# A limit on loads under way, block-key scores in one matmul per head, and one-matmul fillers in an attention and MLP kernel

## The chip, the cores and the metric

The kernel runs on one core of a Trainium2 chip. The metric is device time in microseconds, the median of several executions. One more execution is recorded by the hardware profiler; all views below are of that one.

## The reference

Local attention is followed by a gated MLP and a second MLP, all in float32, with 2 batches, 8 heads, 768 positions and a head size of 64. Each query sees the keys nearer than 16 positions and, beside them, 24 block keys (the maximum over each block of 32 keys) with block means of the values:

```
k_sum = k.reshape(B, H, nb, block, D).max(axis=3)
v_sum = v.reshape(B, H, nb, block, D).mean(axis=3)
scores_l = where(|i - j| < window, scale * q @ k.T, -1e9)
scores_s = scale * q @ k_sum.T + log(block)
a = softmax(concat([scores_l, scores_s]))
x = a @ concat([v, v_sum])                    # to 1536 tokens of 512
xn = x / sqrt(mean(x * x) + 1e-6) * rms_g
x = (silu(xn @ w_gate) * (xn @ w_val)) @ w_out          # 512 -> 1536 -> 512
out = (s * relu(x @ w_in) ** 2 + b) @ w_out2            # 512 -> 2048 -> 512
```

## The kernel before

**Attention.** The 2 x 768 queries are 12 tiles of 128 queries, and a tile is two halves of 64 queries (index c), so that each half needs one window of 96 keys. For a tile `do_qk` (L513) computes all scores: 8 heads are 4 pairs (index j) on the two halves of the partitions (index g), and a head's row holds 96 key columns and 24 block-key columns. Per pair it issues four 64x64 matmuls over the key columns (two g by two c) and then four 64x64 ones over the block-key columns (`km`), which all go to the two PSUM banks of g (L522). Then, for each g, DVE adds the mask and takes the maximum (`do_top`, L541), ACT takes the exponential (L548), PE transposes the result (L559), ACT copies it out of PSUM (L569), PE multiplies with the values (L578), and ACT, GpSimd and DVE divide by the sum (L587 to L596). Each tile ends with its RMS norm (L611 to L619), transposes (L627) and a split into a high and a low F32R part (L638, L640).

**Loads.** All loads are issued by SP on one queue, in order: `load_k` (L273, four strips of keys a batch), `load_q` (L440, one a tile, three buffers), `load_v` (L277, the value windows), `load_vt` (L290, values for the block means), `spread_v` (L312, copies of the block means within SBUF), `load_small` (L157) and `w_load` (L199, raw weights as 64-bit words into three buffers). DVE reduces K strips to `km` (L284) and the value strips to block sums (L294). Output stores are at L860.

**Weights.** Each unit of weights is rebuilt from its 64-bit words by ACT and DVE (L205, L214 to L216) and split into high and low F32R parts (L227, L231). The matmuls of the MLPs take three products of these (L726, L727, L730, and L849 to L852).

**Order.** `plan` (L429) lists the attention work, the first nine weight units and the first matmuls of the gated MLP as tasks with a cost, dependencies and a rank; `give_out` (L328) walks a modelled clock and issues on each engine, as it comes free, the ready task of the lowest rank. That fixes each engine's order when the program is built; on the chip each engine runs its order as semaphores allow. Where the modelled PE would idle for more than `IDLE`, four transposes of the identity into a free bank are issued as a filler (L413 and L414). After the plan the rest of the MLPs follows in a fixed loop order (`moe`, L762). In the model SP runs ahead of the loads by at most `AHEAD` (L380), which sets the place of loads in the order, and no wait.

Of the kernel before, what the change touches and what calls it, by code (L numbers as in the profile page):

```python
# [11 lines left out]
I32 = mybir.dt.int32  # L12
# [6 lines left out]
NB, NH, SEQ, HD = 2, 8, 768, 64  # L19
# [5 lines left out]
NS = SEQ // BLK  # L25
HQ = 64
VH = 66
KW = HQ + 2 * WIN
KC = KW + NS
# [6 lines left out]
NSUB = NB * SEQ // SUB  # L36
TPS = SUB // 128
HEAD = 3
LAT = 0.09
AHEAD = 4.0  # L40
IDLE = 0.6
PTENG = ("ACT",)
QB = 3
# [11 lines left out]
def kernel(ctx: ExitStack, tc: tile.TileContext, q_t, k_t, v_w, v_t, w_gate, w_val, w_out, w_in2, w_out2, vecs, out):  # L55
    nc = tc.nc
# [44 lines left out]
    ident = const.tile([128, 128], F32, name="ident")  # L101
# [4 lines left out]
    vec = const.tile([128, DM + 2], F32, name="vec")  # L106
    gbc, sbc, bbc = vec[:, 0:DM], vec[:, DM:DM + 1], vec[:, DM + 1:DM + 2]
    junk = const.tile([128, DM], mybir.dt.bfloat16, name="junk")
    qc = [const.tile([128, NPAIR, 2, HQ], F32, name=f"q{i}") for i in range(QB)]
# [8 lines left out]
    vt0 = xyp.tile([128, 2 * KD * SUB], F32, tag="xy", name="vt")  # L118
# [4 lines left out]
    kst = [t[:, 0:NPAIR * KL].rearrange("p (j s) -> p j s", j=NPAIR) for t in kb]  # L123
    vst = [[t.rearrange("p (s h d) -> p s h d", s=NTL, h=NH) for t in ts]
           for ts in ([t[:, 0:VT] for t in vb], [part[:, i * VT:(i + 1) * VT] for i in range(2)])]
    km = [const.tile([128, NPAIR, NS], F32, name=f"km{b}") for b in range(NB)]
# [21 lines left out]
    def consts_mask2():  # L148
# [3 lines left out]
        for i, p0, o in ((0, 0, 0), (2, 64, HQ + WIN)):  # L152
            nc.gpsimd.tensor_copy(masks[i], m)
            nc.gpsimd.memset(masks[i][p0:p0 + 64, o:o + WIN], NEG / scale)

    def load_small():
        nc.sync.dma_start(out=vec, in_=vecs)  # L157


    later = [[] for _ in range(8)]  # L160
# [22 lines left out]
    units = []  # L183
# [12 lines left out]

    def w_load(i):
        t = rawp.tile([128, 512, 2], I32, tag="raw", name="raw")
        nc.sync.dma_start(out=t.rearrange("p f c -> p (f c)"), in_=units[i].bitcast(I32))  # L199
        raw_t[i] = t  # L200

    def w_scale(i):
# [67 lines left out]


    def load_k(b, j):
        nc.sync.dma_start(out=kst[b][:, j], in_=k_t[b, j])  # L273

    def load_v(b, s0, n):
        t = vst[b][s0 // NTL][0:KW, s0 % NTL:s0 % NTL + n]
        nc.sync.dma_start(out=t.rearrange("p s h d -> p (s h d)"), in_=v_w[b, s0 // n])  # L277

    def ones_v(b, s0, n):
        rows = KC if s0 < (4 if b == 0 else 2) else KW  # L280
# [6 lines left out]
    vs = vt0[:, NPAIR * SEQ:NPAIR * SEQ + 512]  # L287

    def load_vt(b, j):
        nc.sync.dma_start(out=vt0[:, j * SEQ:(j + 1) * SEQ], in_=v_t[b, j])  # L290

    def sum_vt(b, j):
        c0 = j * 128 + KW
# [15 lines left out]
    def spread_v(b, s0, n):  # L309
        a = vst[b][0][KW:KC, 0:2].rearrange("p (o e) h d -> p o (e h d)", o=1).broadcast_to([NS, n // 2, 2 * NH * VH])  # L310
        o = vst[b][s0 // NTL][KW:KC, s0 % NTL:s0 % NTL + n]
        nc.sync.dma_start(out=o.rearrange("p (o e) h d -> p o (e h d)", e=2), in_=a)  # L312


    tasks = []
# [12 lines left out]
    def give_out():  # L328
        count = {k: 0 for k in rings}
        freed = {k: 0 for k in rings}  # L330
        done_at = {k: [] for k in rings}
        bank_free = [(0.0, i) for i in range(8)]
        used_caps = {k: [] for k in caps}
        pending = {e: [] for e in ("PE", "DVE", "ACT", "POOL", "SP")}
        for i, t in enumerate(tasks):
            pending[t["eng"]].append((t["rank"], i, t))
        for p in pending.values():
            p.sort(key=lambda z: z[:2])
        clock = dict.fromkeys(pending, 0.0)
        dma = 0.0  # L340
        now = 0.0
        left = len(tasks)

        ends = {k: {} for k in rings}

        def ring_ok(k):
            n = rings[k]
            c = count[k]
            return c < n or (c - n in ends[k] and ends[k][c - n] <= now)

        while left:
            moved = False
            for e in ("SP", "PE", "ACT", "DVE", "POOL"):
                if clock[e] > now + 1e-9:
                    continue
                for z in pending[e]:
                    t = z[2]
                    if any(d["end"] is None or d["end"] + LAT > now + 1e-9 for d in t["deps"]):
                        continue
                    if not all(ring_ok(k) for k in t["take"]):  # L360
                        continue
                    b = None
                    if t["bank"]:
                        if sum(1 for x in used_caps[t["bank"]] if x["freed"] is None or x["freed"] > now) >= caps[t["bank"]]:
                            continue
                        ok = [x for x in bank_free if x[0] <= now]
                        if not ok:
                            continue
                        b = min(ok)
                        bank_free.remove(b)  # L370
                        t["b"] = b[1]
                        t["freed"] = None
                        used_caps[t["bank"]].append(t)
                    t["slot"] = {}
                    for k in t["take"]:
                        t["slot"][k] = count[k]
                        count[k] += 1
                    if e == "SP":
                        dma = max(dma, now + 0.5) + t["us"]
                        clock[e] = max(now + 0.06, dma - AHEAD)  # L380
                        t["end"] = dma + 1.3
                    else:
                        clock[e] = now + t["us"]
                        t["end"] = clock[e] + (0.06 if e == "PE" else t["more"])
                    for k, o in t["give"]:
                        ends[k][o["slot"][k]] = t["end"] + LAT
                    for o in t["free"]:
                        o["freed"] = t["end"] + LAT
                        bank_free.append((o["freed"], o["b"]))
                    t["at"] = now  # L390
                    if b is not None:
                        t["fn"](b[1])
                    else:
                        t["fn"]()
                    pending[e].remove(z)
                    left -= 1
                    moved = True
                    break
            if moved:
                continue  # L400
            nxt = [c for c in clock.values() if c > now + 1e-9]
            nxt += [x[0] for x in bank_free if x[0] > now]
            nxt += [v for k in rings for v in ends[k].values() if v > now]
            nxt += [t["end"] + LAT for t in tasks if t["end"] is not None and t["end"] + LAT > now + 1e-9]
            assert nxt, [z[2]["why"] if "why" in z[2] else (e, z[0]) for e in pending for z in pending[e][:3]]
            now = min(nxt) + 1e-6
            at = clock["PE"] + IDLE
            if now > at and any(x[0] <= at for x in bank_free) and ident_at[0]["end"] is not None and ident_at[0]["end"] + LAT < at and pending["PE"]:

                now = at  # L410
                i = min(bank_free)[1]
                ps = bank(i)
                for k in range(4):  # L413
                    nc.tensor.transpose(ps[:, k * 128:(k + 1) * 128], ident, ident)  # L414
                clock["PE"] = now + 0.44

    def dve(n):
# [11 lines left out]
    def plan(x):  # L429
# [7 lines left out]
            K[b, j] = task("SP", mb(128 * KL * 4), lambda: load_k(b, j), rank=rank)  # L437

        def load_q(i):
            nc.sync.dma_start(out=qc[i % QB].rearrange("p j c q -> p (j c q)"), in_=q_t[i])  # L440

        def lq(i, rank, deps=()):
            Q[i] = task("SP", mb(128 * 512 * 4), lambda: load_q(i), deps, rank=rank)
# [60 lines left out]
        box = {}  # L504
        def tile_of(n, i):
            b, t = divmod(i, NTL)
            if i >= 2:
                lq(i, n - 5, [qk[i - QB]] if i >= QB else ())

            def hold(bk):  # L510
                box["S", i, 0] = bank(bk)

            def do_qk(bk):  # L513
                box["S", i, 1] = bank(bk)
                sm_of[i] = smallp.tile([128, 2, NH], F32, tag="sm", name="sm")
                four = [(g, c) for g in range(2) for c in range(2)]
                for j in range(NPAIR):
                    for o, n in ((0, KW), (KW, NS)):
                        for g, c in four:
                            p = slice(64 * g, 64 * g + 64)  # L520
                            k0 = 64 * (2 * t + c)
                            nc.tensor.matmul(box["S", i, g][64 * c:64 * c + 64, j * KC + o:j * KC + o + n], qc[i % QB][p, j, c],  # L522
                                             km[b][p, j] if o else kst[b][p, j, k0:k0 + KW], start=True, stop=True)
            deps = [Q[i], *[KM[b, j] for j in range(NPAIR)], *([qk[i - 1]] if i else ())]
            A0 = task("PE", 0.0, hold, deps, n + 1.2, bank="S")
            A1 = qk[i] = task("PE", 1.25, do_qk, [*deps, A0], n + 1.2, bank="S", take=("sm",))
            box["A0", i] = A1
            return A0, A1

        for n, (i, g) in enumerate(us):  # L530
            b, t = divmod(i, NTL)
# [30 lines left out]
            e = PTENG[n % len(PTENG)]  # L562
# [55 lines left out]
            S = task("POOL", 0.75, do_ss, [R], n - 2)  # L618
# [22 lines left out]
            h = task("ACT", act(512), lambda f=two_x: f(0), [ET], n - 1.2)  # L641
# [27 lines left out]
        for s in range(NSUB):  # L669
            for j in range(HEAD):  # L670
                rk = FR[s] + j * FS
                got = {}
                for k in range(2):
                    ps = []
# [268 lines left out]
```

## Time and profile before

| | us |
|---|---|
| median of 3 runs | 648.09 |
| lowest and highest of them | 647.77, 649.55 |
| the profiled execution, its own time | 647.01 |
| its span between first and last instruction | 645.20 |
| PE busy | 622.8 |
| DVE busy | 378.1 |
| ACT busy | 259.8 |

Attention takes the first 110 us, the first three column blocks of the gated MLP beside it; the MLPs alone take the rest. Engines are PE (matmuls), PEld (weight loads of PE), DVE, ACT, POOL (GpSimd) and SP, whose queue issues the DMAs. "Idle" of an engine is put down to the one that ended it. A view by stretches gives each engine's busy time with the number of its instructions in parentheses, the granted clock of PE (1.00 is 2.4 GHz, 0.50 is 1.2 GHz), the mean busy share of the DMA engines and GB/s.

### The profile page before, as it was taken

The page shows a single profiled execution, that of the slowest core. Times are in us where ns is not written, and L with a number is a line of the kernel's source. Part 1 is how long each engine was busy: PE and PEld are TensorE (multiplying, and loading weights), DVE is VectorE, ACT ScalarE, POOL GpSimd, SP SyncE. Part 2 cuts the span into 40 slices and gives each one's busy share as a digit, 9 for nine tenths or more (in the row PEclk, how much of TensorE's full clock was granted, in tenths as well). Part 3 has the DMA queues.
Part 4 walks back from the last instruction along what each step waited for, and adds up shares of the span by engine and source line. Part 5 has one row for each costly group of instructions (what it writes and reads, how often), then busy time and mean ns, then how long its engine had stood idle before and what let it go on. Part 6 is the DMA issues. An engine that isn't in the chain of part 4 may idle for free.

```text
span 645.2 us, 9632 instructions
## 1 busy us (share of the span) xinstructions
PE 622.8 (97%) x3816; PEld 514.3 (80%) x3816; DVE 378.1 (59%) x731; ACT 259.8 (40%) x524; POOL 141.7 (22%) x159
## 2 busy tenths in 40 slices
PE   5588999999999999999999999999999999999998
PEld 3576788888888888888888888888888888888886
DVE  5469886325851555544556767870388457845532
ACT  2576986334433333212333345542554045404400
POOL 2253856322311111111111111100221022103100
PEclk9889999999999999999999999999999999999999
DMA  9979622003440112221122212230212321210022
GB/s 294 230 264 257 193 60 74 1 1 98 131 130 28 42 63 66 86 61 53 62 65 69 64 65 67 65 100 31 56 46 67 94 62 42 66 61 0 2 98 99
DMA packets 17494, 55.04 MB, mean 85 GB/s; under 512 B 2000, under 2 KB 2256, under 8 KB 17448
## 3 DMA queue, kind: packets, MB, share of 16 engines
q1 hardware_dynamic: 17448, 54.42, 27.7%
q8 instruction: 30, 0.49, 0.3%
q14 instruction: 16, 0.13, 0.1%
HBM read 50.35 MB, written 3.15 MB: 83 GB/s over the span
## 4 chain that ended last, share of the span: by engine, by line
PE 91%; DVE 3%; issue 2%; DMA 1%; ACT 1%; SPq 0%; POOL 0%; POOLq 0%
PE b L726 22%; PE b L730 22%; PE b L727 22%; PE b L852 7%; PE b L850 7%; PE b L849 7%; PE b L559 2%; PE b L522 2%; PE b L578 2%; DMA vt<-in_v_t_dram 1%; PE b L627 1%; DVE vt L294 1%; DVE P L541 0%; DVE km L284 0%; ACT P L548 0%
## 5 line engine op out<-in xcount | busy, mean ns | idle before, releaser
L231 POOL TENSOR_TENSOR wl<-wa,wh 128x512 fp32r<-128x512 f32 x68 | 89.1, 1318 | 389.3 <-ACT wh L227 316.0
L726 PE MATMUL b<-x,wh 128*128 128x512 f32 x288 | 113.7, 395 | 0.1
L727 PE MATMUL b<-x,wl 128*128 128x512 f32 x288 | 112.2, 390 | 0.0
L227 ACT ACTIVATE wh<-wa 128x512 fp32r<-128x512 f32 x68 | 41.5, 627 | 97.2 <-PE b L852 45.5
L730 PE MATMUL b<-x,wh 128*128 128x512 f32 x288 | 77.8, 392 | 0.0
L850 PE MATMUL b<-wl,hg 128*128 128x512 f32 (+1 forms) x196 | 75.1, 385 | 0.0
L849 PE MATMUL b<-wh,hg 128*128 128x512 f32 (+1 forms) x196 | 75.1, 385 | 0.0
L726 PE MATMUL b<-y,wh 128*128 128x512 f32 x192 | 74.7, 389 | 0.0
L727 PE MATMUL b<-y,wl 128*128 128x512 f32 x192 | 74.7, 389 | 0.0
L831 DVE SCALAR_TENSOR_TENSOR b<-u,vec 128x512 f32<-128x512 f32 x48 | 50.7, 1057 | 35.6 <-ACT u L830 35.6
L726 PEld LDWEIGHTS b<-x,wh 128*128 128x128 f32 x288 | 54.1, 188 | 11.3 <-ACT x L638 0.4
L727 PEld LDWEIGHTS b<-x,wl 128*128 128x128 f32 x288 | 54.1, 188 | 10.7
L730 PEld LDWEIGHTS b<-x,wh 128*128 128x128 f32 x288 | 53.5, 188 | 11.0
L726 PE MATMUL b<-hg,wh 128*128 128x512 f32 x144 | 56.0, 389 | 0.0
L727 PE MATMUL b<-hg,wl 128*128 128x512 f32 x144 | 56.0, 389 | 0.0
L751 DVE SCALAR_TENSOR_TENSOR hg<-b,vec,hg 128x512 fp32r<-128x512 f32 x48 | 36.0, 749 | 28.1 <-ACT hg L750 28.1
L852 PE MATMUL b<-wh,hg 128*128 128x512 f32 (+1 forms) x196 | 51.5, 385 | 0.0
L730 PE MATMUL b<-y,wh 128*128 128x512 f32 x192 | 51.3, 389 | 0.0
L216 DVE SCALAR_TENSOR_TENSOR wa<-raw,wa 128x512 int32<-128x512 int32 x68 | 50.0, 735 | 2.0
L750 ACT ACTIVATE hg<-b,vec 128x512 fp32r<-128x512 f32 x48 | 33.0, 687 | 43.0 <-DVE b L831 43.0
L858 DVE TENSOR_TENSOR part<-b,part 128x512 f32<-128x512 f32 (+1 forms) x37 | 24.4, 673 | 43.5 <-PE b L852 43.5
L215 DVE SCALAR_TENSOR_TENSOR wa<-raw,wa 128x512 int32<-128x512 int32 x68 | 47.0, 691 | 2.0
(85 smaller groups left out, 947.2 us busy)
## 6 DMA issues: line engine op xcount, KB each, us to landing
raw<-in_w_out_dram SPq DMA_DIRECT2D x28, 512.0 KB, 3.5
raw<-in_w_in_dram SPq DMA_DIRECT2D x16, 512.0 KB, 4.1
raw<-in_w_gate_dram SPq DMA_DIRECT2D x12, 512.0 KB, 3.6
raw<-in_w_val_dram SPq DMA_DIRECT2D x12, 512.0 KB, 3.6
hg<-in_k_t_dram SPq DMA_DIRECT2D x8, 400.0 KB, 10.0
q<-in_q_t_dram SPq DMA_DIRECT2D x12, 256.0 KB, 7.1
vt<-in_v_t_dram SPq DMA_DIRECT2D x8, 384.0 KB, 8.3
out_dram<-part SPq DMA_DIRECT2D x11, 256.0 KB, 2.0
```

The lines of the kernel that those rows point to most:

```text
L215: lambda: nc.vector.scalar_tensor_tensor(out=ai, in0=hi, scalar=-0x80000000, in1=ai, op0=ALU.bitwise_and, op1=ALU.bitwise_or),
L216: lambda: nc.vector.scalar_tensor_tensor(out=ai, in0=lo, scalar=29, in1=ai, op0=ALU.logical_shift_right, op1=ALU.bitwise_or),
L227: nc.scalar.activation(out=r(h), in_=a_t[i], func=AF.Copy)
L231: nc.gpsimd.tensor_tensor(out=r(lo), in0=a_t.pop(i), in1=high[i], op=ALU.subtract)
L726: nc.tensor.matmul(ps, r(hi[:, kk * 128:(kk + 1) * 128]), xh, start=kk == 0, stop=False)
L727: nc.tensor.matmul(ps, r(lo[:, kk * 128:(kk + 1) * 128]), xh, start=False, stop=False)
L730: nc.tensor.matmul(ps, r(hi[:, kk * 128:(kk + 1) * 128]), r(act(kk, 1)), start=False, stop=kk == 3)
L751: nc.vector.scalar_tensor_tensor(out=r(dst[1]), in0=ps, scalar=bias, in1=dst[0], op0=ALU.add, op1=ALU.subtract)
L831: after(0, lambda u=u, ps=ps: nc.vector.scalar_tensor_tensor(out=ps, in0=u, scalar=sbc[:, 0:1], in1=u, op0=ALU.mult, op1=ALU.mult))
L849: nc.tensor.matmul(acc, gh, r(ws[e][0][:, cs]), start=e == 0, stop=False)
L850: nc.tensor.matmul(acc, gh, r(ws[e][1][:, cs]), start=False, stop=False)
L852: nc.tensor.matmul(acc, r(ge[e][:, 1]), r(ws[e][0][:, cs]), start=False, stop=e == 3)
```

## The change

The three edits are these. Every load that SP issues, and the copies of the block means, go through a new `fetch`, which makes each wait until the fourth one before it has landed (`OUT = 4`); the output stores do not. In `do_qk` the four 64x64 matmuls over the block-key columns of a pair become two, one for each g, with both query halves as 128 weight columns; the key columns stay as they are. A filler becomes one F32 matmul of the identity with itself, repeated to 256 columns, in place of four transposes. Costs and ranks of the planner's tasks are unchanged.

```diff
+OUT = 4
@@
+    sent = []
+
+    def fetch(out, in_):
+
+        d = nc.sync.dma_start(out=out, in_=in_).ins
+        if len(sent) >= OUT:
+            tc.add_manual_dep(d, sent[-OUT].name, mybir.DependencyInfo(mybir.DependencyClass.Sync, mybir.DependencyReason.DATA),
+                              reason="transfers under way")
+        sent.append(d)
+
     def load_small():
-        nc.sync.dma_start(out=vec, in_=vecs)
+        fetch(out=vec, in_=vecs)
...
-        nc.sync.dma_start(out=t.rearrange("p f c -> p (f c)"), in_=units[i].bitcast(I32))
+        fetch(out=t.rearrange("p f c -> p (f c)"), in_=units[i].bitcast(I32))
...
-        nc.sync.dma_start(out=kst[b][:, j], in_=k_t[b, j])
+        fetch(out=kst[b][:, j], in_=k_t[b, j])
...
-                for k in range(4):
-                    nc.tensor.transpose(ps[:, k * 128:(k + 1) * 128], ident, ident)
+                nc.tensor.matmul(ps[:, 0:256].rearrange("p (o c) -> p o c", o=2), ident, ident.rearrange("p (o c) -> p o c", o=1).broadcast_to([128, 2, 128]), start=True, stop=True)
...
-                four = [(g, c) for g in range(2) for c in range(2)]
                 for j in range(NPAIR):
-                    for o, n in ((0, KW), (KW, NS)):
-                        for g, c in four:
-                            p = slice(64 * g, 64 * g + 64)
+                    for g in range(2):
+                        p = slice(64 * g, 64 * g + 64)
+                        S = box["S", i, g]
+                        for c in range(2):
                             k0 = 64 * (2 * t + c)
-                            nc.tensor.matmul(box["S", i, g][64 * c:64 * c + 64, j * KC + o:j * KC + o + n], qc[i % QB][p, j, c],
-                                             km[b][p, j] if o else kst[b][p, j, k0:k0 + KW], start=True, stop=True)
+                            nc.tensor.matmul(S[64 * c:64 * c + 64, j * KC:j * KC + KW], qc[i % QB][p, j, c], kst[b][p, j, k0:k0 + KW], start=True, stop=True)
+                    for g in range(2):
+                        p = slice(64 * g, 64 * g + 64)
+                        nc.tensor.matmul(box["S", i, g][:, j * KC + KW:(j + 1) * KC], qc[i % QB][p, j].rearrange("p c q -> p (c q)"), km[b][p, j], start=True, stop=True)
```

## Rows read from the trace of the kernel before

**Rows 1.** The page: busy time, share and instructions of PE; instruction queue, packets, MB.

```profile
PE 622.8 (97%) x3816; PEld 514.3 (80%) x3816; DVE 378.1 (59%) x731; ACT 259.8 (40%) x524; POOL 141.7 (22%) x159
...
q8 instruction: 30, 0.49, 0.3%
```

**Rows 2.** Stretches: PE, PEld, DVE, ACT, POOL busy, clock, DMA share, GB/s.

```profile
15.00:45.00 30.00, 21.61 (x439) 18.75 (x440) 15.61 (x77) 18.84 (x55) 9.90 (x18) 0.83 0.98 274
45.00:70.00 25.00, 21.19 (x358) 17.12 (x357) 24.62 (x70) 18.26 (x49) 13.20 (x18) 1.00 0.84 227
70.00:110.00 40.00, 40.00 (x584) 32.27 (x583) 32.39 (x124) 33.60 (x95) 24.84 (x32) 1.00 0.32 96
110.00:640.00 530.00, 530.00 (x2346) 439.00 (x2345) 296.20 (x438) 185.74 (x321) 89.89 (x70) 1.00 0.19 61
```

**Rows 3.** The chain that ended last, in order of time: start, us, what.

```profile
20.60 2.25 issue
...
28.26 4.58 issue
...
40.70 0.84 issue
```

**Rows 4.** Stretches that end in the second and third of these waits.

```profile
20.70:28.50 7.80, 5.41 (x125) 4.86 (x126) 4.15 (x31) 5.13 (x18) 2.15 (x8) 0.78 1.04 192
28.50:41.20 12.70, 7.65 (x126) 6.40 (x125) 5.38 (x31) 6.99 (x22) 5.14 (x7) 0.73 1.03 346
```

**Rows 5.** DMA view, instruction packets of 20.1 to 21.7, 30.0 to 31.6, 38.9 to 40.3.

```profile
q8 instruction: 1, 0.02, 4.9%
...
q8 instruction: 1, 0.02, 5.2%
...
q8 instruction: 1, 0.02, 4.6%
```

**Rows 6.** DMA view of 4.9 to 37.6 us: count, KB each, median us to landing.

```profile
hg<-in_k_t_dram SPq DMA_DIRECT2D x4, 400.0 KB, 11.2
q<-in_q_t_dram SPq DMA_DIRECT2D x6, 256.0 KB, 9.2
```

**Rows 7.** Line L273, the K strips issued at 0.73 and at 23.62 us.

```profile
DMA to landing us min/median/max: 3.0/3.0/3.0
...
DMA to landing us min/median/max: 12.5/12.5/12.5
```

**Rows 8.** Timeline of SP's queue: start, us, line, out<-in, count.

```profile
23.62 0.33 SPq L273 DMA_DIRECT2D hg<-in_k_t_dram  x1
```

**Rows 9.** Stretches of low granted clock; columns as in the stages.

```profile
23.30:26.60 3.30, 3.30 (x54) 2.91 (x50) 2.13 (x17) 1.72 (x5) 0.27 (x2) 0.50 1.07 169
...
30.10:36.90 6.80, 4.05 (x35) 3.47 (x35) 2.01 (x11) 2.27 (x7) 1.01 (x1) 0.50 1.03 326
```

**Rows 10.** Timeline of DVE, first block maxima of the second batch.

```profile
43.36 0.94 DVE L284 TENSOR_REDUCE km<-hg 128x24 f32<-128x768 f32 x1
```

**Rows 11.** DMA view of 61 to 72 us, the data queue: packets, MB, share.

```profile
q1 hardware_dynamic: 856, 2.57, 87.2%
```

**Rows 12.** Line L522 in a stretch, scores of one tile: PE, PEld, clock, DMA.

```profile
82.76:84.02 1.26, 1.25 (x64) 1.22 (x64) 1.00 0.00 0
```

**Rows 13.** Timeline of PE, 83.3 to 85.6 us: start, us, line, tile, shapes, count.

```profile
83.63 0.38 PE L522 MATMUL b<-hg,q 64*64 64x96 f32 x8
83.83 0.26 PE L522 MATMUL b<-km,q 64*64 64x24 f32 x8
84.02 0.66 PE L627 MATMUL b<-ident,xn 128*128 128x128 f32 x4
84.61 0.69 PE L578 MATMUL b<-part,PT 120*64 120x66 f32 x16
85.22 0.50 PE L726 MATMUL b<-x,wh 128*128 128x512 f32 x1
```

**Rows 14.** Timeline of PE, two fillers.

```profile
51.86 1.04 PE L414 MATMUL b<-ident 128*128 128x128 f32 x8
```

More of the change, by code (lines that the diff above doesn't have):

```diff
@@ L272, in load_k @@
     def load_k(b, j):
-        nc.sync.dma_start(out=kst[b][:, j], in_=k_t[b, j])
+        fetch(out=kst[b][:, j], in_=k_t[b, j])
     def load_v(b, s0, n):
         t = vst[b][s0 // NTL][0:KW, s0 % NTL:s0 % NTL + n]
-        nc.sync.dma_start(out=t.rearrange("p s h d -> p (s h d)"), in_=v_w[b, s0 // n])
+        fetch(out=t.rearrange("p s h d -> p (s h d)"), in_=v_w[b, s0 // n])
     def ones_v(b, s0, n):
@@ L289, in load_vt @@
     def load_vt(b, j):
-        nc.sync.dma_start(out=vt0[:, j * SEQ:(j + 1) * SEQ], in_=v_t[b, j])
+        fetch(out=vt0[:, j * SEQ:(j + 1) * SEQ], in_=v_t[b, j])
     def sum_vt(b, j):
@@ L311, in spread_v @@
         o = vst[b][s0 // NTL][KW:KC, s0 % NTL:s0 % NTL + n]
-        nc.sync.dma_start(out=o.rearrange("p (o e) h d -> p o (e h d)", e=2), in_=a)
+        fetch(out=o.rearrange("p (o e) h d -> p o (e h d)", e=2), in_=a)
     tasks = []
@@ L439, in load_q @@
         def load_q(i):
-            nc.sync.dma_start(out=qc[i % QB].rearrange("p j c q -> p (j c q)"), in_=q_t[i])
+            fetch(out=qc[i % QB].rearrange("p j c q -> p (j c q)"), in_=q_t[i])
         def lq(i, rank, deps=()):
```

## The prediction

> **What bounds the kernel now.** I read the page first, then the stages, then the chain of waits. PE is busy 97% of the span [rows 1], and the stages show where it is not [rows 2]: from 70 to 640 us it is busy without a gap, so there the end moves only with PE's own work. What PE loses before its tail lies ahead of 70, and behind the first loads it is 8.4 us of the 30 from 15 to 45 and 3.8 of the 25 from 45 to 70, where DVE is busy 24.6 of 25 and sets the pace. So I ask what holds the stretch 15 to 45. In the chain it is mostly "issue", time in which the engine waits for nothing that the profile names: 2.25 us at 20.60, 4.58 at 28.26 and 0.84 at 40.70, 7.67 us together [rows 3].
>
> What is "issue"? Between the first and the second of these waits PE and PEld start 125 + 126 = 251 instructions, between the second and the third 251 again [rows 4]. A pause after a fixed number of instructions looks like a block of program that has not come. Queue 8 moves instructions, 30 packets of 0.49 MB, 16 KB each; with 3816 matmuls and as many weight loads that is one packet for some 255 [rows 1]. One such packet lies at 20.1 to 21.7 us, one at 30.0 to 31.6, one at 38.9 to 40.3 [rows 5]; PE goes on at 22.85, 32.84 and 41.54, each time just over a microsecond behind its packet. The trace does not show when a packet was asked for. If it is when the block before it begins, at 22.85 and 32.84, the next ones stood 7.2 and 6.1 us in line.
>
> In line behind what? From 4.9 to 37.6 us 27 loads and copies are issued (the counts of the view added; two of its rows stand), one per 1.2 us, and q and K take 9.2 and 11.2 us to land [rows 6]: 10 / 1.2, about eight under way. A lone K strip lands in 3.0 us [rows 7]. DMA is busy 0.98 of the time [rows 2], so the loads queue, and I read the instruction packets as queueing with them. The rule in the Trainium skill, "Runtime: NRT & Kernel Launch", section "Instruction fetch mechanics", is that crossing the boundary of a block of 256 instructions is "mostly hidden". The trace agrees on the block's size and differs on the cost, 7.67 us; by the page the limit would bring nothing.
>
> **The change, part by part.**
>
> *Four transfers under way.* A load now waits on SP until the fourth before it has landed. All that is behind it on SP's queue waits too: the loads of q, K, v, v_t and the weights' raw tiles, and the SBUF copies of the block means; for these wait, in turn, PE's scores, DVE's block maxima and sums, and ACT's scaling. Data are not moved later by that as long as the DMA engines have work: they are the bound there. Four are enough if moving four takes longer than one alone takes from issue to landing: 4 x 1.2 = 4.8 us against 3.0 plus one issue of 0.33 [rows 6 to 8]. An instruction packet should meet half the line: 7.2 and 6.1 become some 3.3 us, and with 1.4 for the packet and 1.3 until PE moves, 6.0 us. The second block ran 5.4 us (22.85 to 28.26), but will hold more work, since the scores need a quarter fewer instructions and, below, more time. So I take the three waits to go whole: 7.67 us.
>
> With them goes the slow clock. PE's granted clock is 0.50 (1.2 GHz) from 23.3 to 26.6 and from 30.1 to 36.9, each just behind or within a wait, and PE is busy 3.30 + 4.05 = 7.35 us in these [rows 9]. At 2.4 GHz that would be half: 3.7 us. Together 11.3 us are on offer.
>
> They can't all be had, since next come the loads, which go no faster. The second batch's K strip issued at 23.62 lands 12.5 us later, at 36.1, and DVE reads it at 43.36 [rows 7, 8, 10]: 7.2 us of slack. So the cap is 7.2 us, less what the limit costs in DMA pace. That cost no row shows. From below it is 0 (by the 4.8 above; a gain is excluded, since the engines are full). From above, take 61 to 72 us, where fewer loads are queued and the queue's share is 87% [rows 11] instead of 98% [rows 2], partly since SP had nothing to send: 11 points, or 3.4 of the 31 us from 5 to 36. I take 1.0, nearer the lower end, since SP's own waits explain part of that stretch. Gain: 6.2 us, range 3.8 to 7.2.
>
> The MoE stage loses nothing: it has three raw tiles, so no more than three loads can be under way there. The output stores are not limited.
>
> *Block columns in one matmul.* Per head pair, four 64*64 matmuls over 24 columns become two 64*128 ones; each F32 matmul is two PE instructions and two weight loads, so a tile's scores go from 64 + 64 instructions to 48 + 48. They take 1.25 us a tile now [rows 12]. While the shape stays, PE starts the next group 0.18 us before the last one ends: the key columns end at 83.63 + 0.38 = 84.01, the block columns begin at 83.83. Where the shape changes it is 0.07: the block columns end at 84.09, the 128*128 transposes begin at 84.02; these end at 84.68, the 120*64 matmuls begin at 84.61; these end at 85.30, the 128*128 ones begin at 85.22 [rows 13]. The last pair differs in columns alone and pays as well. So a change of shape costs 0.11 us, and the new code has seven more of them a tile (four into 64*128, three back): 0.77 us. No row shows 64*64 against 64*128. From below: no such cost, and fewer instructions, near 0. From above: each pass over 24 columns with the wide weights takes as long as one of the wide transposes, 0.66 / 4 = 0.165 [rows 13]: two per pair are 0.33 where the narrow group takes 0.19 (83.83 to 84.02), 4 x 0.14 = 0.56 more, 1.3. I take 0.77, since every change of shape in the rows pays its 0.11, and 24 columns are far from 128. The Trainium skill says the same in "TensorEngine Tiling (Array Packing)", section "Key Properties": changing the tiling mode drains the engine; its "Available Configurations" list 64*64 and 64*128 as two modes. The trace agrees where it has a change (0.07 against 0.18), and the rule speaks against this edit.
>
> Where does it count? The scores of tiles 8 to 11, at 70.2, 82.8, 86.3 and 91.5 us (one of four rows alike stands), lie in PE's full stretch [rows 2, 12]: 4 x 0.77 = +3.1 us. Those of tiles 6 and 7 lie where PE idles 3.8 us beside DVE: 0. Those of tiles 1 to 5 (3.9 us) eat of the surplus in the first part, 11.3 - 3.9 = 7.4, still above the cap of 7.2; without that surplus they would cost up to 3.9. Tile 0 waits for its loads anyway.
>
> *Fillers.* 13 fillers of four transposes become one F32 matmul of 256 columns, two instructions. Now: half of the 1.04 us that eight take, 0.52 with the tail [rows 14]. Then: the nearest F32 rows are the two passes of 96 columns, one group from 83.63 to 83.83, 0.20, so 0.53 for 256; one F32R step of 512 columns, as many as two passes of 256, has 0.50 with its tail [rows 13]. So 0 to within 0.02 each. Only the last stands at the edge of PE's full stretch; the others fill waits for DVE or ACT. I take 0.
>
> *Sum.* 6.2 - 3.1 = 3.1 us less. The profiled execution took 647.0 us (span 645.2), 1.1 below the median of the runs, 648.1; 643.9 of its kind is **645.0** as a median. 0.3% is 1.9 us, about what a measurement of this kernel can tell from no change.
>
> **The rivals.**
>
> *No drain.* If 64*64 and 64*128 can follow each other like one shape, the 3.1 us are not paid, and tiles 1 to 5 leave the surplus whole: 6.2 to 7.2 us less, 641.4. For it: both use 64 rows, and no row has this pair. Against it: 120*64 to 128*128 [rows 13].
>
> *Half the line is not short enough.* The request may come later than I think, or four loads may make a long line still. If half of the 7.67 us stays, 3.8 is gained and 3.1 paid: 647.4, no difference. For it: PE ran the second block in 5.4 us, and a packet needs 6.0. Against it: a block will hold more work.
>
> *The engines starve (slower).* With four under way, any time that SP spends on another wait leaves fewer queued; the copies of the block means move on 24 partitions and the q loads are the smallest, just ahead of the K strips with their 7.2 us of slack. If the pace of loads up to 36 us falls by 13% (4.1 us), the gain equals the 3.1 us of the scores; at 20% (6.2 us) 1.0 is gained and 3.1 paid: 650.2. For it: 87% where fewer are queued [rows 11]. Against: the 4.8 against 3.3.
>
> *The waits are not for program.* If "issue" has another cause, the limit leaves it, and the 3.1 us are paid: 651.2. For it: no row shows a request. Against: 251 instructions twice, each with its packet [rows 4, 5]. By the page on instruction fetch this would be the case.
>
> **How the numbers follow.** Forecast (drain paid, waits gone, gain 5 to 7): 0.52, from 644.2 to 646.4, with its own bounds of a tile's cost 643.5 to 647.0; no drain 0.18; half the waits stay 0.17; starved 0.09; not for program 0.04. Faster by over 0.3% (below 646.2): 0.43 of the forecast, the 0.18, and 0.03 of the third: 0.64. Same: 0.25, the rest of the forecast (0.09), 0.14 of the third and 0.02 of the starved. Slower: 0.11. The range leaves out the far ends of the rivals: 640.8 to 649.8.
>
> **What would show it.** The three "issue" waits gone or under 1 us together; granted clock 1.00 from about 17 us on; K strips landing 4 to 6 us after issue with DMA's share still near 1.0 until 36 us; PE full from about 64 us instead of 70; scores of 2.0 us a tile with ends overlapping 0.07 at each change of shape. Scores of 1.25 us would mean no drain; a DMA share under 0.9 before 36 us, with DVE waiting on K or PE on q, would mean starving; "issue" waits of the old length would mean that they are not what I read.

## The result, and the profile after

The changed kernel takes 650.94 us (median of 7 executions, 650.28 to 658.12) where the kernel before took 648.64 (7, 647.77 to 649.55) on the same chip: ratio 1.0054, 95% interval 1.0032 to 1.0077. By that ratio it is slower by 0.54%; the medians are 2.3 us apart, where the forecast was a gain of 3.1 us. The profiled execution took 650.54 us, 3.5 more than that of before. In the kernels here with the new scores in all tiles, 7 of 55 executions took 657.7 to 658.3 us, at a mean granted clock of 1.00, none of them with a trace, and no other kernel has one above 654.5.

The page of the changed kernel, in the columns of [rows 1] (busy, share, instructions), with its line for the instruction queue and its loads of K and q (count, KB each, median us from issue to landing):

```profile
PE 636.4 (98%) x3598; PEld 519.7 (80%) x3598; DVE 378.2 (58%) x731; ACT 260.0 (40%) x524; POOL 140.9 (22%) x159
...
q8 instruction: 28, 0.46, 0.3%
...
hg<-in_k_t_dram SPq DMA_DIRECT2D x8, 400.0 KB, 4.6
q<-in_q_t_dram SPq DMA_DIRECT2D x12, 256.0 KB, 4.8
```

PE has 218 instructions fewer and is busy 13.6 us more. A K strip now lands in 4.6 us, and two instruction packets are spared. The stages, in the columns of [rows 2]:

```profile
15.00:45.00 30.00, 28.96 (x426) 22.41 (x427) 19.57 (x84) 21.71 (x65) 12.44 (x21) 1.00 0.96 288
45.00:70.00 25.00, 23.68 (x279) 17.55 (x277) 23.39 (x79) 17.90 (x47) 13.10 (x20) 1.00 0.94 255
70.00:110.00 40.00, 40.00 (x469) 31.16 (x468) 27.70 (x105) 30.87 (x86) 19.92 (x24) 1.00 0.24 75
```

From 15 to 45 us PE idles 1.0 us where it idled 8.4 [rows 2], at a granted clock of 1.00 where it had 0.83, with the loads as fast as before (share 0.96, 288 GB/s against 274). Yet the end comes later. What PE waits for up to 110 us, as the list of its waits has it (total, times, longest):

```profile
PE b L532 <- DMA q<-in_q_t_dram: 4.6, 1, 4.6
PE b L532 <- DMA hg<-in_k_t_dram: 1.7, 1, 1.7
PE b L590 <- ACT PT L581: 1.5, 4, 0.5
PE b L535 <- DVE km L295: 0.4, 1, 0.4
PE b L590 <- POOL sm L602: 0.3, 1, 0.3
```

No "issue" is left of the 7.67 us of [rows 3]. What PE did with the time must then be in the scores. The timeline of PE, tile 9 (L532 key columns, L535 block columns), in the columns of [rows 13]:

```profile
82.14 0.40 PE L532 MATMUL b<-hg,q 64*64 64x96 f32 x8
82.47 0.41 PE L535 MATMUL b<-km,q 64*128 64x24 f32 x4
82.80 0.40 PE L532 MATMUL b<-hg,q 64*64 64x96 f32 x8
...
84.45 0.41 PE L535 MATMUL b<-km,q 64*128 64x24 f32 x4
84.78 0.66 PE L639 MATMUL b<-ident,xn 128*128 128x128 f32 x4
```

From the tile's first matmul to the next operation it is 84.78 - 82.14 = 2.64 us, 0.66 for each of four pairs. Before it was 1.25 [rows 12]. The new scores cost **1.40 us a tile** with a quarter fewer instructions; the prediction said 0.77. The block columns of a pair now hold PE for 0.33 (82.47 to 82.80). Before, they held it for 0.19 at the end of a tile (83.83 to 84.02) [rows 13], where a change of shape follows, and inside a tile for 0.09, as the timeline of the kernel before has it:

```profile
82.98 0.26 PE L522 MATMUL b<-km,q 64*64 64x24 f32 x8
83.07 0.38 PE L522 MATMUL b<-hg,q 64*64 64x96 f32 x8
```

And the chain that ended last, for the stretch in which the prediction saw the loads as the limit (start, us, what):

```profile
20.16 0.33 PE b L532 x8
20.49 0.34 PE b L535 x4
...
22.15 1.08 PE b L590 x32
23.23 0.33 PE b L532 x8
...
25.54 0.34 PE b L535 x4
25.87 1.02 PE b L571 x8
26.89 0.33 PE b L532 x8
...
29.20 0.33 PE b L535 x4
29.54 0.64 PE b L590 x16
```

From 20.16 to 30.18 the chain is PE's own work, and most of it is scores: not the loads and not a wait, but the tiles that were to "eat of the surplus".

### The profile page after: what moved, and what is told of

Read it like the earlier page. It is cut to its first block, busy times and chain, and to the rows that moved or that the text cites. A ratio compares the mean times of both kernels' runs of the same rounds, so it can differ in the third digit from the quotient of the medians.

```text
span 648.8 us, 9192 instructions
## 1 busy us (share of the span) xinstructions
PE 636.4 (98%) x3598; PEld 519.7 (80%) x3598; DVE 378.2 (58%) x731; ACT 260.0 (40%) x524; POOL 140.9 (22%) x159
## 4 chain that ended last, share of the span: by engine, by line
PE 97%; ACT 1%; DMA 1%; issue 0%; DVE 0%; POOL 0%; SPq 0%
PE b L738 22%; PE b L742 22%; PE b L739 22%; PE b L864 7%; PE b L862 7%; PE b L861 7%; PE b L535 3%; PE b L532 2%; PE b L590 2%; PE b L571 2%; PE b L424 1%; DMA hg<-in_k_t_dram 1%; PE b L639 1%; ACT PT L581 0%; PE b L310 0%
```

## The experiments

Each ratio is to the kernel before, measured in the same comparison. Where two kernels are set against each other, the text says whether they shared a comparison.

**Each edit alone.** The first kernel has only the limit:

```diff
+OUT = 4
@@
+    def fetch(out, in_):
...
+        if len(sent) >= OUT:
...
```

> Only the limit of four transfers; scores and fillers as before. Theory (instruction packets queue behind loads): the three issue waits of 7.67 us are gone although PE has as many instructions as before, granted clock 1.00 from about 17 us on, K strips land in about 5 us, and with the old scores the gain reaches its cap: 5 to 8 us less than before, 641 to 644. Rival (the waits went because the scores need a quarter fewer instructions): the waits are still there, 4 us or more together, and the time is within 2 us of before. Rival (four transfers starve the DMA engines): K strips are used later than before, DMA share under 0.9 from 5 to 35 us, 648 or more.

Measured: 641.07 us (639.97 to 645.05, 6 executions), ratio 0.9895, 0.9865 to 0.9926. Its stage from 15 to 45 us, a wait of PE that has grown (1.4 us in all before), the only "issue" wait up to 110 us, and the stretch in which its clock is low:

```profile
15.00:45.00 30.00, 25.45 (x531) 20.61 (x530) 22.51 (x87) 21.87 (x65) 12.96 (x22) 0.89 0.94 275
...
PE b L589 <- ACT PT L580: 3.3, 3, 2.0
...
PE b L589 <- issue: 0.2, 1, 0.2
...
37.40:44.20 6.80, 6.48 (x88) 5.62 (x86) 6.65 (x11) 4.23 (x12) 3.85 (x5) 0.50 0.96 337
```

The waits that the prediction read as waits for program go, though this kernel has as many instructions as before. Little of the clock comes back in this trace: 6.48 us of PE's work lie at 0.50 (37.4 to 44.2), where it was 7.35 [rows 9]. Tile 8 begins at 64.44 us against 70.2 before, 5.8 earlier, and so it stays to the end. The chain that ended last shows what stops it there:

```profile
4.43 5.16 DMA vt<-in_v_t_dram
9.60 5.46 DMA vt<-in_v_t_dram
15.09 5.89 DMA hg<-in_v_w_dram
20.99 5.91 DMA hg<-in_v_w_dram
27.30 6.46 DMA hg<-in_v_w_dram
```

From 4.4 to 33.8 us it is loads, one behind the other: the cap that the prediction had put on the gain, though it had read it from the K strips, and these are loads of v_t and v.

The second kernel has only the new scores, with loads unlimited:

```diff
-                    for o, n in ((0, KW), (KW, NS)):
-                        for g, c in four:
...
+                    for g in range(2):
...
+                        nc.tensor.matmul(box["S", i, g][:, j * KC + KW:(j + 1) * KC], qc[i % QB][p, j].rearrange("p c q -> p (c q)"), km[b][p, j], start=True, stop=True)
```

> Only the block-key edit; eight transfers under way as before, old fillers. Theory (the shape change and the wide weights cost 1.4 us a tile, of which four tiles lie in PE's full stretch, and the waits for program stay, only at other places since a block now holds more work): 5.6 us for the four tiles, and issue waits of 4 to 8 us still there: 652 to 656. Rival (fewer instructions are what removed the waits): issue waits under 1 us, and the time is that of all three edits, 650 to 651.

Measured: 651.96 us (649.49 to 658.28, 12), ratio 1.0061, 1.0035 to 1.0086. Its stage:

```profile
15.00:45.00 30.00, 29.20 (x427) 23.37 (x428) 19.35 (x82) 21.31 (x63) 12.36 (x20) 0.94 1.01 281
```

Here too no "issue" is left among PE's waits up to 110 us, with eight loads under way as before; 4 to 8 us of it were expected, and the rival's sign (under 1 us) came true. I read it so: a block of program with the new scores lasts long enough for its successor to come, since they are fewer instructions and slower ones; which of the two does it, no run tells. So the limit and the new scores each take the same waits away: one has the time back, the other works through it.

The third has only the fillers (one matmul of 256 columns for four transposes).

> Only the one-matmul fillers. Theory A (a filler costs 0.1 us more at the low clock and nothing otherwise, and the wait for program hides that): 648 to 649.5, no difference. Theory B (the four fillers ahead of the first transposes put the block means 0.5 us or more later, and the granted clock rises later than 16.4 us): the multiplication with the values of tile 0 starts 0.5 to 1.5 us later than 18.58 and the time is up to 1.5 us longer.

Measured: 647.61 us (644.57 to 651.74, 12), ratio 0.9986, 0.9964 to 1.0008: no difference. It tells something else as well. PE's waits in it, and its stretch ahead of the first of them beside the same stretch of the kernel before (the second fence; PE, PEld with their counts, as in [rows 2]):

```profile
PE b L577 <- issue: 3.8, 1, 3.8
PE b L521 <- issue: 1.4, 1, 1.4
...
0.00:22.00 22.00, 14.84 (x222) 10.52 (x222) 11.82 (x39) 7.22 (x18) 4.79 (x25) 1.00 0.95 288
```

```profile
0.00:20.60 20.60, 13.30 (x222) 10.20 (x222) 11.45 (x35) 6.87 (x16) 4.86 (x25) 1.00 0.93 288
```

The first wait comes 1.4 us later in time, and behind 222 + 222 instructions in both, although other operations have been done by then. The wait follows the number of instructions.

**How many under way.** Only `OUT` is changed, in the kernel with the limit alone.

> Old scores and fillers, at most six transfers under way where four gave 641.1 and eight (before) 648.6. If instruction packets stand in line behind the loads, the line is three quarters of before: the waits at instruction counts 449 and 705 come back in part, 1 to 4 us together, packets start between those of before and of four, and the time lies between: 643 to 646.5. If the line does not matter, but some other effect of the limit did: 641 or 648.6.

> Old scores and fillers, at most three transfers under way. If the loads are the bound behind the limit (a lone load takes 3.0 us, three at 1.2 us each move in 3.6), the engines begin to starve: DMA share from 15 to 35 us below 0.94, K strips of the second batch later than 35 us, and 642 to 646. If pace is still full, shorter lines bring nothing more, since the waits are gone already: 640 to 642.

> The limit alone at five under way. Six gave 644.8 and four 641.1. Theory (what remains of the line sets the waits, the engines are still full at four): between the two, 642 to 644.5. Rival: four already lets the engines run dry at times, and five is the best: below 641.

> The limit of four alone, once more, with more executions, beside the three kernels below. Theory: 641 to 642, since the first comparison had six executions from 640.0 to 645.1. Rival: those six were low, and twelve give 643.5 or more; then the late tiles' cost of 8.4 us in medians comes down to the 5.6 that the profiles show.

| under way | us, median | ratio, 95% interval | K strip to landing, page, us | "issue" of PE to 110 us, us |
|---|---|---|---|---|
| 8 (before) | 647.6 to 648.6 | | 10.0 | 7.9 |
| 6 | 644.82 | 0.9949, 0.9930 to 0.9967 | 6.8 | 4.9 |
| 5 | 643.48 | 0.9927, 0.9905 to 0.9948 | 6.0 | 6.6 |
| 4 (again) | 641.77 | 0.9911, 0.9887 to 0.9936 | 6.0 | 1.6 |
| 4 | 641.07 | 0.9895, 0.9865 to 0.9926 | 4.9 | 0.2 |
| 3 | 647.15 | 0.9990, 0.9966 to 1.0013 | 3.7 | 0.2 |

The stages from 15 to 45 us at six and at three:

```profile
15.00:45.00 30.00, 25.95 (x518) 22.09 (x516) 20.08 (x90) 23.29 (x69) 12.48 (x21) 0.89 1.03 277
```

```profile
15.00:45.00 30.00, 24.70 (x526) 20.59 (x526) 20.62 (x84) 22.66 (x65) 13.22 (x22) 0.89 0.82 238
```

With fewer under way the time falls down to four, and the waits with it by and large (one execution each; five had more of them than six). They do not price the gain one for one: at five 6.6 of 7.9 us were left, and the median is 4.3 us lower. Nor are they always gone at four: of other kernels with the limit and the old scores in the early tiles, limit_fill has 2.6 us of them and limit_late 3.1. At three the waits are gone as well, but the time is above the expected 642 to 646, and the DMA share falls from 1.03 to 0.82 and 277 GB/s to 238: that is the rival of the starving engines, and four (0.94, and 0.91 in limit_again) is just short of it. `limit_again` came out at 641.77, so the gain of the limit alone is 6 to 7.5 us.

**What a tile's scores cost.** `limit_apart` has the limit, the old fillers, and the same 24 matmuls a tile in another order: all 16 of the key columns, then all 8 wide ones. So it has one change of shape within a tile, where the new scores have seven.

```diff
                 for j in range(NPAIR):
                     for g in range(2):
...
                             nc.tensor.matmul(S[64 * c:64 * c + 64, j * KC:j * KC + KW], qc[i % QB][p, j, c], kst[b][p, j, k0:k0 + KW], start=True, stop=True)
+                for j in range(NPAIR):
                     for g in range(2):
...
```

> The limit with old fillers, and scores with wide block-key matmuls as in the change, but a tile's 16 key-column matmuls all come first and its 8 wide ones behind them, so there is one change of shape inside a tile and not seven. If the change of shape is nearly all of the 1.4 us (7 x 0.2): a tile takes about 1.4 us. If the wide weights are: seven changes at 0.11 were 0.77 and the rest, 0.63, stays, so a tile takes 1.9 to 2.0 us. In time: the kernel with the limit alone plus four times what a tile takes over 1.25 us: +0.6 or +2.6 to 3.0 us.

Measured: 645.49 us (642.34 to 649.25, 12), ratio 0.9964, 0.9938 to 0.9990, 4.4 us above `limit` in one comparison. The timeline of its tile 10:

```profile
81.53 0.89 PE L533 MATMUL b<-hg,q 64*64 64x96 f32 x32
82.35 1.08 PE L537 MATMUL b<-km,q 64*128 64x24 f32 x16
83.35 0.50 PE L740 MATMUL b<-x,wh 128*128 128x512 f32 x1
```

A tile takes 83.35 - 81.53 = 1.82 us; 1.4 or 1.9 to 2.0 was expected, by which of the two terms it is, and it is both. Six changes of shape fewer save 2.64 - 1.82 = 0.82: 0.14 each in the mean, where the prediction had 0.11. The 16 wide passes take 1.00 (82.35 to 83.35, with the change behind them), 0.0625 each, in place of 32 narrow ones. Against the old 1.25 this order is 0.57 more, of which one added change of shape is 0.14; the rest, some 0.43, goes to passes over 24 columns that now come with 128 weight columns. So the 1.40 is 7 x 0.137 = 0.96 for the shape and 0.43 for the passes. The split supposes that a pass takes as long in either order. The prediction took the first term alone. In time, four tiles at 0.57 are 2.3 us; the 4.4 between the medians is more, but the two intervals leave room for 2.3.

`late_8` has no limit, the old fillers, and the new scores in tiles 8 to 11 alone:

```diff
+                if i >= 8:
+                    for j in range(NPAIR):
+                        for g in range(2):
...
+                else:
+                    four = [(g, c) for g in range(2) for c in range(2)]
...
```

> No limit, old fillers, the new scores in tiles 8 to 11 alone. Theory: all else is the kernel before, so its three waits stay and each late tile adds 1.40 us: 5.6 above before, 653.5 to 654. Rival: the late tiles cost more than their time on PE, by what comes behind them: over 655. The prediction's price of 0.77 a tile would give 3.1 above before, 651.

Measured: 653.38 us (651.63 to 654.41, 6), ratio 1.0082, 1.0062 to 1.0103: 5.6 us slower, 4 x 1.40. Its profile agrees on the waits (5.8 and 2.1 us of "issue"). Its span is 7.4 us longer than that of before, since it shows one thing more, a stretch behind tile 8 with PE busy and the clock low, which by 4 x 0.43 costs an estimated 1.7 us:

```profile
73.00:77.00 4.00, 4.00 (x18) 3.43 (x19) 2.63 (x12) 1.60 (x5) 1.47 (x3) 0.57 0.23 66
```

**Where the cost is paid.** `limit_scores` and `limit_scores_2` are one kernel, run twice: the limit and the new scores with the old fillers. `limit_early` has the limit and the new scores in tiles 0 to 7, `limit_late` the limit and the new scores in tiles 8 to 11, and `early_8` the new scores in tiles 0 to 7 without the limit (the condition is `i < 8` in place of `i >= 8`).

> The limit and the block-key edit, old fillers: the change without its fillers. The limit alone came to 641.1, the scores alone to 652.0, all three to 650.9. Theory A (both remedies take away the same waits for program, so the limit adds nothing to slow scores, and the fillers cost little): 649.5 to 651.5. Theory B (the one-matmul fillers ahead of the first transposes cost the front of the kernel 1.4 us or more, which reaches the end): 647 to 649.

> The limit, the old fillers, and the new scores in tiles 0 to 7 alone. Theory: 641.07 + 2.6 = 643.7, the rest of what the kernel with both edits lost; in the profile PE is at most 3 us later than in the kernel limit when tile 8 begins, though the eight tiles hold 8 x 1.4 = 11.2 us more of PE's time. Rival (my prediction's reading, a surplus that takes the cost whole): 641. Rival (nothing is taken): 641.07 + 9.8 = 651.

> The limit, the old fillers, and the new scores in tiles 8 to 11 alone; tiles 0 to 7 keep the narrow ones. Limit alone had 641.07, limit with the new scores in all tiles 649.23, 8.2 more. Theory: a tile in the stretch where PE is full pays 1.40 us, four of them 5.6, so this kernel comes out at 646.7 and the profile shows the end moved back by 5.6 against the kernel limit, 1.4 at each of the four tiles; the other 2.6 us belong to tiles 1 to 7, which is 0.4 of 1.4 for each. Rival: the early tiles carry most of the 8.2, since they delay DVE's work behind them too; then this kernel is below 644.

> No limit, old fillers, the new scores in tiles 0 to 7 alone. Theory: a block of instructions lasts longer by the slower scores, so the waits go as in the kernel with the new scores in all tiles (651.96 against 648.6): that less the late tiles' 5.6 is 646.4, faster than before, and the profile has no issue wait of over 0.5 us ahead of 70 us. Rival (the slower scores are only a cost): 649 or more.

| kernel | us, median (range, executions) | ratio, 95% interval |
|---|---|---|
| limit_scores | 649.23 (647.24 to 658.07, 12) | 1.0017, 0.9996 to 1.0038 |
| limit_scores_2 | 649.37 (648.07 to 658.14, 12) | 1.0028, 1.0012 to 1.0044 |
| limit_early | 644.25 (642.57 to 652.00, 12) | 0.9953, 0.9930 to 0.9977 |
| limit_late | 649.46 (645.72 to 652.48, 12) | 1.0025, 1.0005 to 1.0046 |
| early_8 | 647.23 (643.85 to 652.45, 12) | 0.9995, 0.9968 to 1.0022 |

Eight early tiles hold 8 x 1.40 = 11.2 us more of PE's work. Without the limit they cost nothing that 12 executions can tell (early_8, 0.9968 to 1.0022): the work goes into the time of the waits. With the limit, the gain of 6.0 to 7.5 falls to 3.3 (0.9953 against 0.9895 and 0.9911, in other comparisons: 2.7 to 3.8 us). PE's rows from 15 to 45 us, early_8 with its only "issue" wait first, limit_early second:

```profile
15.00:45.00 30.00, 27.53 (x377) 22.03 (x376) 16.30 (x77) 19.30 (x58) 10.14 (x18) 0.89 1.01 274
...
PE b L523 <- issue: 1.7, 1, 1.7
```

```profile
15.00:45.00 30.00, 28.60 (x456) 23.18 (x456) 21.66 (x85) 22.17 (x65) 13.36 (x22) 1.00 0.97 290
...
65.88 0.43 PE L545 MATMUL b<-hg,q 64*64 64x96 f32 x6
```

In early_8, PE is busy 27.53 of the 30 us where it had 21.61 [rows 2], and 1.7 us of issue waits are left of 7.67 (none above 0.5 was expected). In limit_early it is busy 28.60, and tile 8 begins at 65.88, 4.3 us ahead of before, where the limit alone was 5.8 ahead, and 4.8 in limit_again (65.41).

`limit_late` is at 649.46, not at the 646.7 that was expected. Its profiled execution, 645.72 us, does what the theory says. The timeline where its tile 8 begins:

```profile
63.33 0.51 PE L534 MATMUL b<-hg,q 64*64 64x96 f32 x8
```

That is 6.9 us ahead of the kernel before (70.2), and its span of 643.9 us ends 1.3 ahead of that one's 645.2: 5.6 us are lost in between, over four tiles. But its executions fall into two groups. Five with a mean granted clock of 0.997 to 1.00 took 645.7 to 647.7, seven with 0.989 to 0.995 took 649.2 to 652.5. The five lie around the expected 646.7 (median 646.76). The group means of the clock differ by 0.007, which over 645 us of a busy PE is an estimated 4.4 us, about what lies between the groups (3.8); what makes the clock fall in this kernel is open. The low stretch behind tile 8 in late_8, above, may be the same thing; none of the seven left a trace, so this can't be settled.

**The fillers with the rest.** `limit_fill` is the limit and the new fillers; `whole_2` is the whole change once more, in one comparison with limit_scores_2, which differs from it in the fillers alone.

> The limit and the one-matmul fillers, old scores. The fillers alone made no difference that 12 runs could tell (0.9986, 0.9964 to 1.0008). If they are neutral: 640 to 643, as the limit alone. If the front's 1.4 us reach the end once the waits for program no longer hide them: 642.5 or more.

> The limit and the new scores with the old fillers once more, beside the whole change on one chip, so that the fillers' share of the whole change is measured in one comparison. Theory: the new fillers cost 1 to 2 us, so this kernel is that much below the one beside it, near 649.2. Rival (the prediction's term of 0): no difference between the two.

> The whole change, unaltered, beside the kernel with its limit and scores alone. Theory: 651, 1 to 2 us above that one, with the first transposes and the first product with the values over 1 us later in the profile. Rival: the two are the same within 0.3%, and the late start of the whole change's profile was that one execution's granted clock.

Measured: limit_fill 642.48 us, ratio 0.9914, 0.9884 to 0.9945, like the limit alone. whole_2 650.14 us (12), 1.0030, 1.0010 to 1.0051; limit_scores_2 beside it 1.0028. The expected 1 to 2 us for the fillers isn't there: 0.8 between the medians, within the error. In the profiled execution of the changed kernel the first transposes began 1.4 us later than before (16.30 against 14.87); in that of whole_2 they began at 16.21, 0.5 later than in limit_scores_2 (15.67) and not over 1, and the whole is 1.2 us shorter than in the changed kernel. Tile 8 begins at 67.01 in whole_2 and at 66.77 in limit_scores_2. Nothing here contradicts the prediction's 0, but a cost of up to some 1.5 us is within the error.

## Why the prediction was wrong, step by step

**The waits are for program: right.** They follow a count of instructions (fill), they shrink with the loads ahead (eight, six, four; five breaks the row), and they go when a block lasts longer (scores). No trace shows a request, so this stays a reading, the one that fits all three. That the limit takes them whole held with the new scores; with the old ones 0.2 to 3.1 us are left in four traces. By the Trainium skill, "Runtime: NRT & Kernel Launch", section "Instruction fetch mechanics", crossing a block's boundary is "mostly hidden". The trace differs, on this reading: here it cost up to 4.58 us [rows 3], and the kernel with 0.2 to 1.6 us of these waits left is 1% faster. "Not for program" and "half the line is not short enough" have fallen.

**The limit's gain: right.** 6.2 us, range 3.8 to 7.2, was forecast; alone it gave 6.0 and 7.5 in two comparisons. The cap was right in size and partly in place: loads in a row hold the end, but those of v_t and v and not K's. The pace lost was small, as taken (DMA share 0.94 and 0.96). Of the clock's 3.7 us little came back in the trace of the limit alone (6.48 us of work at 0.50 for 7.35), and all in that of the changed kernel; so it is the cap that made the sum right, and not both terms under it.

**The scores: the step that failed.** 0.77 us a tile was forecast, with 1.3 as the upper bound; 1.40 was measured. The change of shape was found from the rows and was of about the right size (0.14 for 0.11). The second term, wide weights over 24 columns, stood in the upper bound only (0.77 + 0.56 = 1.3) and was taken as 0, since "24 columns are far from 128". It is 0.43. That it lies below the 0.56 is luck, for the 0.56 was miscounted: a pair has two wide matmuls of two instructions each, so four passes and not two, and the narrow group takes 0.09 inside a tile and not 0.19. By four passes of 0.165 the prediction's own bound is about 3.0 us a tile, and not 1.3.

**What that did to the sum.** The term enters it twice. In tiles 8 to 11 it is 4 x 1.40 = 5.6 in place of 3.1, as late_8 shows. And in tiles 1 to 5 it is 7.0 in place of 3.9: of the 11.3 us on offer 4.3 are left, not 7.4, and that is below the cap. So the gain falls from 6.2 to 4.3, and limit_early agrees (3.3 in its median; tile 8 ahead by 4.3 in its profile, though two traces of one kernel, limit_scores and limit_scores_2, differ there by 1.6). With the right price the prediction's own working gives -4.3 + 5.6 = +1.3, or 649.4 as a median; measured 650.94 and 650.14. The remainder of about 1 us in the medians no run settled. In the profile of the changed kernel tile 8 is ahead by only 2.0, and two of its steps lay on the chain there that the prediction called free, tile 0's scores ("waits for its loads anyway") and the first fillers; the second fence is the timeline of PE in the kernel before, its first four fillers:

```profile
9.00 0.53 PE b L532 x8
9.53 0.55 PE b L535 x4
...
13.65 1.24 PE b L424 x2
...
16.30 1.94 PE b L571 x8
...
19.09 0.53 PE b L532 x8
```

```profile
10.09 4.63 PE L414 MATMUL b<-ident 128*128 128x128 f32 x16
```

Here a filler takes 1.24 us (0.70 at 67.55) where it took 4.63 / 4 = 1.16 before. And all of PE is slow here for longer: eight key-column instructions take 0.53 until 19.6 and 0.33 from 20.16, where the kernel before is at its later pace from 17.05 on; the view by stretches gives a clock of 1.00 for both. That differs between executions of one kernel: the eight transposes of tile 0 take 1.06 us in limit_scores and 1.94 in limit_scores_2, and tile 8 begins at 65.15 and 66.77. So much of the 2.3 us by which the changed kernel's tile 8 is behind that of limit_early may be this one execution's.

**Surplus.** The prediction held that early tiles are free as long as they eat of a surplus. The mechanism holds (early_8 costs nothing for 11.2 us of work), but it makes the slow scores a second remedy for the same waits. The forecast sat 1.2 us from the edge of that surplus (7.4 against 6.2), and an error of 0.25 us a tile was enough to cross it. The upper bound of 1.3 was carried through tiles 8 to 11 alone (647.0 at most); in tiles 1 to 5 it would have left 11.3 - 6.5 = 4.8, and the sum -4.8 + 5.2, no gain at all.

**The fillers: 0, not contradicted. No drain: wrong** (0.07 of overlap at a change between 64*64 and 64*128, as 82.14 + 0.40 against 82.47 shows, and not the 0.18 of one shape). **The engines starve: wrong at four, right at three.** By the Trainium skill, "TensorEngine Tiling (Array Packing)", section "Key Properties", a change of tiling mode drains the engine. The trace agrees that each change costs, 0.14 us in the mean.

The best of these kernels is the one with the limit of four alone: 641.07 and 641.77 us, 1% below the kernel before.

## What to carry to other kernels

Where PE pauses with nothing to wait for, count the instructions between pauses, and if they match a block of program, let as few loads be under way as keep the DMA engines full: here four, and three were too few. Fewer matmuls aren't less time: price a merged one by its changes of shape plus its passes at the new weight width, both together, in every place where PE is the bound. And when an edit adds work "in the time of a wait" that another edit removes, work the sum out at both ends of the added work's price, since past the edge of the surplus each further microsecond is paid in full.

## What the hardware showed that was not expected

PE's clock fell to 0.57 from 73 to 77 us in late_8 while PE was busy 4.00 us of 4, right behind tile 8's scores. The low stretches of the kernel before lie at or behind a wait of PE (23.3 to 26.6 and 30.1 to 36.9 us [rows 9]), and that of the kernel with the limit (37.4 to 44.2) follows its wait of 2.0 us. In the profiled execution of the changed kernel, where PE hardly waits, the clock is 1.00 in all three stages. But waits alone do not decide it: limit_late idles 5.5 of the 30 us from 15 to 45 at a clock of 1.00.
